# A decode kernel's TensorE program made shorter: looped query projection and query broadcasts, the broadcasts moved behind the MLP's first layer, and branch hints at the end of two engines' programs

## The chip, the cores and the metric

One core of a Trainium2 chip (trn2). The metric is the device time of one execution in microseconds, lower is better. Before: 1292.9 us (median of three: 1292.82, 1292.90, 1293.01).

Ratios between two kernels are computed as the mean time of one kernel's runs over that of the other's runs of the same rounds, so they are not quite the ratio of the medians quoted beside them.

## The reference, cut to what matters

One decode step for batch 8: attention over a key and a value cache beside an MLP, both on a layer norm of the same `x`.

```python
xn = layernorm(x)                                 # (8, 1, 576)
q  = (xn @ wq).reshape(B, 1, 32, 128)             # 32 heads of 128
p  = softmax(einsum(q, k_cache) * 128**-0.5)      # k_cache, v_cache: (8, 32, 4096, 128) bf16
a  = einsum(p, v_cache).reshape(B, 1, 4096) @ wo
h  = gelu(layernorm(xn) @ w1 + b1)                # 576 -> 4608
return x + a + h @ w2 + b2
```

The caches are 2 x 268 MB and are read once. Everything else is small.

## The kernel before: the parts that matter

The cache goes through in 32 tiles. Each tile has one key load and one value load of 8 MB (64 KB on each of 128 partitions), all issued by SyncE on one DMA queue into a ring that also holds, at the start, the weights and scratch of the head. The head is everything ahead of the first tile: layer norms, query projection, query broadcasts, the MLP's first layer with its activation, and a turn of the hidden vector.

```python
# SyncE's order of loads (cut)
load wq; load w1; load_kv(k_v, 0, 0)              # issued at once, traffic until about 44 us
wait(wq_read, head_done); load_kv(v_v, 0, 1)      # value load 0
wait(mlp_done)                                    # the next keys overwrite w1 and the head's scratch
for t in range(1, NT):
    sy.wait_ge(sem["kf"], NX * (t - 1) + 2)       # two key blocks of tile t-1 are used
    load_kv(k_v, t, 0)
    sy.wait_ge(sem["vf"], t)                      # values of tile t-1 are used
    load_kv(v_v, t, 1)
```

So the load of keys 1 waits for the start of tile 0, and the load of values 1 for its end. From tile 1 on, the tiles wait for their keys instead: VectorE's wait for keys is 281.3 us in 31 pieces, the longest 9.1 us (list of waits).

```python
# TensorE in the head (cut)
def queries(e):                                   # 36 matmuls, 32 columns each, four side by side
    for c in range(WC):
        for m in range(M):
            e.matmul(S_ps[0][m*MP:(m+1)*MP, :], lhsT=xT[:, c, :], rhs=wv[:, m], ...)
...
for b in range(B):                                # broadcasts: 8 x 4 matmuls, 64 columns each
    for v in range(2):
        for k in range(NG):
            e.matmul(t[k*M*QP:(k+1)*M*QP, v*NH2:(v+1)*NH2, :], lhsT=sel[:, v*B+b], rhs=q_v[:, k], ...)
    # ScalarE copies the bank to qb
... then the first layer, waiting for w1; activation; turn; then VectorE's first key product
```

The softmax here doesn't subtract the row's maximum and nothing guards it: scores larger than these inputs give would overflow.

Of the kernel before, what the change touches and what calls it, by code (L numbers as in the profile page):

```python
# [3 lines left out]
ALU = mybir.AluOpType  # L4
# [5 lines left out]
P = 128  # L10
# [4 lines left out]
QP = P // G  # L15
# [99 lines left out]
def later(src, dst, engine):  # L115

    ins = list(src.instructions)
    wait = next(i for i in ins if i.engine == engine and type(i).__name__ == "InstEventSemaphore")
    assert not dst.instructions
    src.instructions = [i for i in ins if i is not wait]  # L120
    dst.instructions = [wait]


def decode(nc, A_x, A_k_cache, A_v_cache, A_wq, A_wo, B_x, B_w1, B_b1, B_w2, B_b2, out):
# [68 lines left out]
    bv = sb("bv", [2, MP], BF16)  # L193
# [25 lines left out]
    HS, HJ = 3, 2  # L219
    HK = R // (HS * HJ)  # L220
    assert HS * HJ * HK == R and HK * P <= NB
# [4 lines left out]
    xT = early(0, [P, WC, MP])  # L226
    sel = early(0, [P, 2 * B, M, QP])
    q = early(0, [P, NB])
    yT = early(1, [P, WC, MP])
    b1r = early(1, [2, HF])  # L230
    t1s = [early(1, [HS * MP, HK, P], FP32) for _ in range(HJ)]
    hs = [early(1, [HS * MP, HK, P]) for _ in range(HJ)]
# [7 lines left out]
    o_ps, tot_ps, oT_ps = bank("o_ps"), bank("tot_ps"), bank("oT_ps")  # L240
    acc = [bank(f"acc{m}") for m in range(NO)]

    names = ["k", "v", "prod", "ebd", "ob", "s", "o", "t", "sc", "x", "rec", "kf", "vf", "on", "end", "out"]
# [4 lines left out]

    def block(name, eng=ENG.PE):

        nc.enter_bb(name, parent=main, valid_engines=[eng])

# [32 lines left out]
    od.op("gpsimd", [], ["xT"], lambda e: e.memset(xT, 0.0))  # L285
    od.op("gpsimd", [], ["yT"], lambda e: e.memset(yT, 0.0))
    od.op("gpsimd", [], ["bv"], lambda e: e.memset(bv[:], 0.0))
# [74 lines left out]

    def queries(e):
        for c in range(WC):
            wv = wq_sb[:, c, :].rearrange("p (x m d) -> p m x d", m=M, d=Dh)
            for m in range(M):
                i = e.matmul(
                    S_ps[0][m * MP:(m + 1) * MP, :], lhsT=xT[:, c, :], rhs=wv[:, m],
                    start=(c == 0), stop=(c == WC - 1))
        return i  # L370
# [15 lines left out]
    q_v = q.rearrange("r (n k d) -> r k n d", n=NH2, k=NG)  # L386
    for b in range(B):
        ps, key = (tot_ps, "tot") if b % 2 else (oT_ps, "oT")
        t = ps.rearrange("p (g d) -> p g d", d=Dh)

        def broadcast(e, t=t, b=b):
            for v in range(2):
                for k in range(NG):
                    i = e.matmul(
                        t[k * M * QP:(k + 1) * M * QP, v * NH2:(v + 1) * NH2, :],
                        lhsT=sel[:, v * B + b].rearrange("p m q -> p (m q)"), rhs=q_v[:, k],
                        start=True, stop=True)
            return i

        pe(["q", "sel"], [key], broadcast)  # L400
        dst = qb[:, b * NHG:(b + 1) * NHG, :]
        act([key], [f"qb{b}"], lambda e: e.activation(out=dst, in_=t, func=ACT.Copy))

# [3 lines left out]
    h_ps = [p[:HS * MP, :HK * P].rearrange("p (k r) -> p k r", k=HK) for p in (o_ps, S_ps[2])]  # L407

    def layer(e, lhsT, rows, **flags):
        wv = rows.rearrange("x (p r) -> x r p", r=R)  # L410
        for j in range(HJ):
            for s in range(HS):
                r0 = (s * HJ + j) * HK
                i = e.matmul(  # L414
                    h_ps[j][s * MP:(s + 1) * MP], lhsT=lhsT, rhs=wv[:, r0:r0 + HK, :], **flags)
        return i
# [4 lines left out]
    pe(["bv", "b1r"], ["h_ps"], lambda e: layer(e, bv[:], b1r, start=False, stop=True))  # L421
    for j in range(HJ):
        t1, k1, hp, h = t1s[j], f"t1_{j}", h_ps[j], hs[j]
        act(["h_ps"], [k1], lambda e: e.activation(out=t1, in_=hp, func=ACT.Square))  # L424
        dve([k1], [k1], lambda e: e.tensor_scalar(  # L425
            out=t1, in0=t1, scalar1=0.044715, scalar2=1.0, op0=ALU.mult, op1=ALU.add))
        dve([k1, "h_ps"], [k1], lambda e: e.tensor_tensor(out=t1, in0=t1, in1=hp, op=ALU.mult))
        act([k1], [k1], lambda e: e.activation(out=t1, in_=t1, func=ACT.Tanh, scale=GELU_C))
        dve([k1], [k1], lambda e: e.tensor_scalar(
            out=t1, in0=t1, scalar1=1.0, scalar2=0.5, op0=ALU.add, op1=ALU.mult))  # L430
        dve([k1, "h_ps"], [f"h{j}"], lambda e: e.tensor_tensor(
            out=h, in0=t1, in1=hp, op=ALU.mult))
    for j in range(HJ):
        h = hs[j]
        t = S_ps[j][:, :HK * HS * MP].rearrange("p (k n) -> p k n", k=HK)

        def turn(e, h=h, t=t):
            for k in range(HK):
                i = e.matmul(
                    t[:, k, :], lhsT=h[:, k, :], rhs=ident[:HS * MP, :HS * MP],  # L440
# [5 lines left out]
            out=hT_sb[:].rearrange("p (s j k) n -> p j k s n", s=HS, j=HJ)[:, j],  # L446
            in_=t.rearrange("p k (s n) -> p k s n", s=HS)[:, :, :, :2 * B]))
# [51 lines left out]
    ve, sa, te = nc.vector, nc.scalar, nc.tensor  # L499
# [110 lines left out]
    sa.sem_inc(sent)  # L610

# [65 lines left out]
    block("project")  # L677

# [25 lines left out]
    ins.then_inc(sem["end"], 1)  # L704

# [25 lines left out]
```

## Time and profile before

From the page of the kernel before: the span, and part 3, which has for each DMA queue its packets, bytes, and the time that they took as a share of sixteen engines' span.

```profile
span 1291.5 us, 14658 instructions
...
q1 hardware_dynamic: 10368, 556.93, 99.7%
q8 instruction: 3, 0.05, 0.0%
...
q14 instruction: 1, 0.01, 0.0%
```

Queue 1, with all the loads, fills the DMA engines for 99.7% of the span: this kernel is bound by its traffic. I took it that an engine's work costs time only where it delays a load; r5 below agrees, where 11.5 us more work of VectorE cost 4.6 us. The lines "instruction" I read as fetches of program text, since they come and go with the program: with the hints added (r2) queue 8 has two packets instead of three and queue 14 none. They look like nothing, but the packet records below show otherwise.

From the timeline of the kernel before (start us, duration us, engine line operation, tiles, count, and in brackets the idle time before it): the queries, the first and the last four broadcasts, one group of the layer, the first key product, and loads.

```profile
13.84 4.01 PE L367 MATMUL s_ps<-ring 128*32 128x512 bf16 x36 [1.36 <-DVE quad L354]
...
18.55 0.41 PE L394 MATMUL oT_ps<-ring 128*64 128x256 bf16 x4 [0.36 <-ACT ring L385]
...
22.57 0.64 PE L394 MATMUL tot_ps<-ring 128*64 128x256 bf16 x4
...
23.95 0.33 SPq L271 DMA_DIRECT2D ring<-in_A_v_cache_dram  x1
...
26.02 0.85 PE L414 MATMUL o_ps<-ring 128*32 128x384 bf16 x3 [2.80 <-DMA ring<-in_B_w_dram]
...
46.82 6.70 DVE L559 TENSOR_TENSOR ring<-ring,qb 128x4096 bf16<-128x4096 bf16 x3 [0.32 <-DVE hT_sb L445]
...
53.53 0.33 SPq L271 DMA_DIRECT2D ring<-in_A_k_cache_dram  x1
...
74.24 0.33 SPq L271 DMA_DIRECT2D ring<-in_A_v_cache_dram  x1
```

The queries' narrow matmuls start four at a time (the first four within 0.01 us, at 13.84 us), the broadcasts two at a time (the first two within 0.01 us, at 18.55 us). The first layer starts at 26 us because its weights land then (bracket). The broadcasts and ScalarE's copies of them, 18.6 to 23.9 us, lie in that wait. Keys 1 are issued at 53.5 us.

The chain that ended last, in order of time (start us, duration us, what):

```profile
1259.74 28.52 DMA ring<-in_A_wo_dram
1288.26 0.04 issue
1288.31 1.29 PE acc L374 x18
1289.60 0.02 issue
1289.62 0.45 DVE fin L604
```

The time is set by the landing of the last weights; about 4.4 us follow.

**The packet records.** The trace also has each DMA packet's start and duration. A load ends with sixteen packets of 4 bytes (1136 for the 71 loads), which I read as one on each of the sixteen engines, so one can see when each engine finished it. Worked out from these records for the kernel before:

- Steady state: an 8 MB load takes each engine 19.35 us (8.39 MB: 433 GB/s), and load follows load without a gap.
- Thirteen engines finish each load within 0.5 us of one another. Three are 1.2 to 1.4 us behind them, to the end. They fall behind one at a time, each after an instruction fetch: at 29.9 us (queue 8, 16384 bytes, 1.02 us), 52.2 us (queue 14, 8192 bytes, 0.31 us) and 76.0 us (queue 8, 16384 bytes, 1.05 us). The records do not name the engine of a packet; that an engine delayed once stays behind is read from lags that repeat load after load: 1.32, 1.42 and 1.54 us behind the median at 102.5 us, 1.35, 1.45 and 1.57 us at 1244 us.
- The last weights' final packets: thirteen engines by 1287.1 us, the three late ones at 1288.3 to 1288.5 us.

### The profile page before, as it was taken

To read this page: it belongs to the slowest core of one execution; us is meant where nothing else is said; L and a number is where in the kernel's file an instruction comes from. 1 tells how busy PE (TensorE), PEld (TensorE's weight loads), DVE (VectorE), ACT (ScalarE), POOL (GpSimd) and SP (SyncE) were. 2 spreads that over 40 slices of the span, in tenths; PEclk is the share of its full clock that TensorE was granted. 3 is DMA by queue.
4 is the path that set the end of the run, shared out by engine and by line. 5 is a ranking of instruction groups with operands and counts; after the bars stand their busy time and mean duration, and the time that the engine had idled before them with its cause. 6 is when DMAs were issued, how large, how long until landed. Compare 5 with 4: busy or idle time off the path is not lost. (4 is left out here: it accounts for less than half of the span.)

```text
span 1291.5 us, 14658 instructions
## 1 busy us (share of the span) xinstructions
PE 736.8 (57%) x4707; PEld 322.3 (25%) x4707; DVE 829.4 (64%) x740; ACT 56.8 (4%) x181; POOL 2.4 (0%) x12
## 2 busy tenths in 40 slices
PE   4654565554565554665554565554566554565557
PEld 1222232222222222222222232222222222222223
DVE  2655677655677655677655677655677655577654
ACT  2000000000000000000000000000000000000000
POOL 0000000000000000000000000000000000000000
PEclk8778887778887777887777887778887777888779
DMA  9999999999999999999999999999999999999998
GB/s 419 441 427 440 430 428 449 422 428 449 422 428 449 422 430 447 422 436 440 424 436 438 426 438 434 428 442 428 428 449 422 428 449 422 428 449 422 430 447 350
DMA packets 10410, 557.02 MB, mean 431 GB/s; under 512 B 1163, under 2 KB 1188, under 8 KB 1446
## 3 DMA queue, kind: packets, MB, share of 16 engines
q1 hardware_dynamic: 10368, 556.93, 99.7%
q8 instruction: 3, 0.05, 0.0%
q10 hardware_dynamic: 38, 0.02, 0.0%
q14 instruction: 1, 0.01, 0.0%
HBM read 556.94 MB, written 0.01 MB: 431 GB/s over the span
## 5 line engine op out<-in xcount | busy, mean ns | idle before, releaser
L643 PE MATMUL s_ps<-ring,ident 128*128 x2048 | 544.5, 423 | 514.1 <-PEq L641 513.1
L559 DVE TENSOR_TENSOR ring<-ring,qb 128x4096 bf16<-128x4096 bf16 x256 | 579.2, 2283 | 281.6 <-DMA ring<-in_A_k_cache_dram 281.3
L643 PEld LDWEIGHTS s_ps<-ring,ident 128*128 128x128 bf16 x2048 | 217.4, 106 | 828.3 <-issue 678.5
L534 DVE TENSOR_REDUCE sc<-s_ps 128x32 f32<-128x512 f32 x256 | 171.8, 684 | 0.0
L662 PE MATMUL o_ps<-ring,ebd 128*32 128x512 bf16 x2048 | 116.4, 380 | 0.0
L546 DVE TENSOR_TENSOR ebd<-es,head 128x1536 bf16<-128x1536 bf16 x64 | 77.9, 1218 | 0.0
L569 DVE RECIPROCAL rec<-tot_ps 128x8 f32<-128x8 f32 x32 | 6.6, 208 | 110.7 <-PE oT_ps L670 110.7
L582 ACT ACTIVATE es<-sc 128x192 bf16<-128x192 f32 x64 | 19.8, 310 | 1104.2 <-DVE sc L534 1104.2
L662 PEld LDWEIGHTS o_ps<-ring,ebd 128*32 128x32 bf16 x2048 | 51.6, 97 | 62.5 <-issue 13.6
L670 PE MATMUL oT_ps<-selc,ob 128*128 128x8 f32 x256 | 33.9, 259 | 12.3 <-ACT ob L586 12.3
L670 PEld LDWEIGHTS oT_ps<-selc,ob 128*128 128x128 f32 x256 | 31.0, 191 | 15.2 <-ACT ob L586 15.2
L586 ACT ACTIVATE ob<-o_ps 128x512 f32<-128x512 f32 x32 | 19.1, 597 | 80.2 <-PE o_ps L662 80.2
L425 DVE TENSOR_SCALAR ring<-ring 96x384 f32<-96x384 f32 x2 | 0.7, 352 | 26.4 <-ACT ring L424 26.4
L545 DVE TENSOR_TENSOR Es<-Ep 128x1 f32<-128x1 f32 x32 | 5.1, 160 | 13.3 <-ACT es L582 13.3
L666 PEld LDWEIGHTS tot_ps<-headf,Es 128*128 128x128 f32 x64 | 9.5, 187 | 13.6 <-issue 13.6
L666 PE MATMUL tot_ps<-headf,Es 128*128 128x8 f32 x64 | 12.4, 266 | 0.0
L582 ACT ACTIVATION_READ_ACCUMULATOR es<-sc 128x1 f32 x64 | 11.9, 186 | 0.0
L414 PE MATMUL o_ps<-ring 128*32 128x384 bf16 x27 | 7.8, 860 | 2.8 <-DMA ring<-in_B_w_dram 2.8
L574 DVE TENSOR_TENSOR Ox<-on,quad 128x32 bf16 x32 | 6.2, 192 | 4.8
L414 PE MATMUL s_ps<-ring 128*32 128x384 bf16 x27 | 7.9, 862 | 0.0
L374 PE MATMUL acc<-ring,hT_sb 128*8 128x288 bf16 x72 | 6.0, 335 | 2.8 <-DMA ring<-in_B_w_dram 2.8
L336 PE MATMUL tot_ps<-ident,ring 40*128 40x16 bf16 x9 | 0.7, 204 | 11.8 <-DVE ring L314 11.8
(76 smaller groups left out, 61.2 us busy)
## 6 DMA issues: line engine op xcount, KB each, us to landing
ring<-in_B_w_dram SPq DMA_DIRECT2D x2, 5184.0 KB, 25.2
ring<-in_A_wq_dram SPq DMA_DIRECT2D x1, 4608.0 KB, 13.7
ring<-in_A_wo_dram SPq DMA_DIRECT2D x1, 1728.0 KB, 28.6
ring<-in_A_wo_dram SPq DMA_DIRECT2D x1, 1584.0 KB, 26.5
ring<-in_A_wo_dram SPq DMA_DIRECT2D x1, 1008.0 KB, 28.5
ring<-in_A_k_cache_dram SPq DMA_DIRECT2D x32, 31.9
ring<-in_A_v_cache_dram SPq DMA_DIRECT2D x32, 30.5
ring<-in_A_wo_dram SPq DMA_DIRECT2D x1, 288.0 KB, 28.8
```

The source lines that it names most:

```text
L414: i = e.matmul(h_ps[j][s * MP:(s + 1) * MP], lhsT=lhsT, rhs=wv[:, r0:r0 + HK, :], **flags)
L534: ins = ve.tensor_reduce(out=sc[:, n * CB:(n + 1) * CB], in_=bank_of(x).rearrange("p (c d) -> p c d", d=DL), axis=AX.X, op=ALU.add)
L546: ve.tensor_tensor(out=ebd[:, ja:jb], in0=es[:, a:b].rearrange("p (j c) -> p j c", c=4).unsqueeze(2) .to_broadcast([P, nj, G, 4]), in1=hea ...
L559: ve.tensor_tensor(out=k, in0=k, in1=qb[:, bass.ds(t, 1), :].to_broadcast([P, CB, Dh]), op=ALU.mult,).then_inc(sem["prod"], 1)
L569: ve.reciprocal(out=rec[:], in_=tot_ps[:, :G]).then_inc(sem["rec"], 1)
L574: ve.tensor_tensor(out=Ox[:, bass.ds(t, 1)].rearrange("p o g m -> p (o g) m"), in0=on[:].unsqueeze(2).to_broadcast([P, G, M]), in1=quad[:] ...
L582: sa.activation(out=es[:, a * CB:b * CB], in_=sc[:, a * CB:b * CB], func=ACT.Exp, scale=scale, accum_out=Ep[:, i:i + 1]).then_inc(sem["x"], 1)
L586: sa.activation(out=ob[:].rearrange("r c d -> r (c d)"), in_=o_ps, func=ACT.Copy).then_inc(sem["ob"], 1)
L643: ins = te.matmul(to, lhsT=idn, rhs=k[:, :, d * DL:(d + 1) * DL], start=(d == 0), stop=(d == Dh // DL - 1))
L662: ins = te.matmul(o_ps[m * MP:(m + 1) * MP, :], lhsT=ebd[:, j].rearrange("p g c -> p (g c)"), rhs=vals[:, c:c + 4, :], start=(j < M), stop ...
L666: te.matmul(tot_ps[:, :G], lhsT=Es[:].to_broadcast([P, P]), rhs=headf[:], start=True, stop=True).then_inc(sem["vf"], 1)
L670: ins = te.matmul(oT_ps[:, :G], lhsT=ob[:, c, :], rhs=selc[:, c, :], start=(c == 0), stop=(c == 3))
```

## The change

The intent: fewer instructions in TensorE's program, by loops with register addresses in place of unrolled code. The looped matmuls are widened with zeros, the queries to full width; looped matmuls at the old width were not run (r4 and r16 go back to it unrolled). The broadcasts go behind the first layer, where ScalarE and VectorE compute the activation. Two hints name the last branch of VectorE and of TensorE.

```diff
     def queries(e):
-        for c in range(WC):
-            for m in range(M):
-                i = e.matmul(S_ps[0][m * MP:(m + 1) * MP, :], lhsT=xT[:, c, :], rhs=wv[:, m], ...)
+        def part(at, w, start):                     # zeros around the 32 columns: 128 wide
+            for m in range(M):
+                e.matmul(S_ps[0], lhsT=xTz[:, bass.ds(at + (M - 1 - m) * MP, P)], rhs=wv[:, m], ...)
+        part(0, 0, True)
+        (at, w), close = looped("queries", WC - 1, at=(M * MP, M * MP), w=(HQ, HQ))
+        part(at, w, False)
+        close()
 ...
-    for b in range(B): ...                          # 32 unrolled broadcasts, before the layer
     ... first layer (now in groups of 4 x 512 and 1 x 256 columns, not 6 x 384) ...
+    def broadcasts(e):                              # behind the layer, a loop of 8
+        (at,), close = looped("broadcast", B, at=(0, MQ))
+        e.wait_ge(sem["free"], 1).then_inc(sem["free"], -1)
+        for v in range(2):
+            for k in reversed(range(NG)):
+                i = e.matmul(t[:(k + 1) * MQ, v * NH2:(v + 1) * NH2, :],
+                    lhsT=selz[:, bass.ds(at + (v * B + 1 - k) * MQ, (k + 1) * MQ)], rhs=q_v[:, k], ...)
+        i.then_inc(sem["full"], 1)
+        close()
+    ... squares; queries_out(range(2)); tanh ...; queries_out(range(2, B)); turn
 ...
+    vector_last = nc.mark_branch_hint_location(ENG.DVE)     # at the start of VectorE's program
+    ve.br("vector_end").branch_hint(vector_last)            # at its end
+    place = nc.mark_branch_hint_location(ENG.PE)            # at the start of the projection
+    te.br("tensor_end").branch_hint(place)                  # at TensorE's end
```

More of the change, by code (lines that the diff above doesn't have):

```diff
@@ L117, in later @@
     ins = list(src.instructions)
-    wait = next(i for i in ins if i.engine == engine and type(i).__name__ == "InstEventSemaphore")
+    moved = [next(i for i in ins if i.engine == engine and type(i).__name__ == kind)
+             for kind in ("InstDrain", "InstEventSemaphore")]
     assert not dst.instructions
-    src.instructions = [i for i in ins if i is not wait]
-    dst.instructions = [wait]
+    src.instructions = [i for i in ins if i not in moved]
+    dst.instructions = moved
 def decode(nc, A_x, A_k_cache, A_v_cache, A_wq, A_wo, B_x, B_w1, B_b1, B_w2, B_b2, out):
@@ L192, in decode @@
     low = sb("low", [P, MP], BF16)
-    bv = sb("bv", [2, MP], BF16)
     stats = {t: sb(f"stats_{t}", [B, 2, nc.vector.BN_STATS_DIM], FP32) for t in "xy"}
@@ L217, in early, with between @@
         return t
-    HS, HJ = 3, 2
-    HK = R // (HS * HJ)
-    assert HS * HJ * HK == R and HK * P <= NB
+    def between(room, groups, n):
+        pad = (groups - 1) * MP
+        t = early(room, [P, pad + n * groups * MP])
+        return t, t[:, pad:].rearrange("p (c r) -> p c r", c=n)[:, :, :MP]
+    HK = NB // P
+    HG = [(j, s, r, min(r + HK, R)) for n, r in enumerate(range(0, R, HK)) for j, s in [divmod(n, M)]]
+    HJ = HG[-1][0] + 1
+    HN = [[(r0, r1) for j, _, r0, r1 in HG if j == i] for i in range(HJ)]
+    assert all(len({r1 - r0 for r0, r1 in g}) == 1 for g in HN)
+    HR = [(len(g), g[0][1] - g[0][0], g[0][0]) for g in HN]
     x8, b2r = early(0, [B, D]), early(0, [1, D])
@@ L225, in decode @@
     dup = early(0, [YP + B, D, 2])
-    xT = early(0, [P, WC, MP])
-    sel = early(0, [P, 2 * B, M, QP])
-    q = early(0, [P, NB])
+    xTz, xT = between(0, M, WC)
+    MQ = M * QP
+    selz = early(1, [P, (1 + 2 * B) * MQ])
+    sel = selz[:, MQ:].rearrange("p (i m q) -> p i m q", m=M, q=QP)
+    q = early(1, [P, NB])
     yT = early(1, [P, WC, MP])
+    bv = early(1, [2, MP])
     b1r = early(1, [2, HF])
-    t1s = [early(1, [HS * MP, HK, P], FP32) for _ in range(HJ)]
-    hs = [early(1, [HS * MP, HK, P]) for _ in range(HJ)]
+    t1s = [early(1, [n * MP, k, P], FP32) for n, k, _ in HR]
+    hs = [early(1, [n * MP, k, P]) for n, k, _ in HR]
     def bank(name):
@@ L239, in decode @@
     S_ps = [s_all[:, i * NB:(i + 1) * NB] for i in range(NS)]
-    o_ps, tot_ps, oT_ps = bank("o_ps"), bank("tot_ps"), bank("oT_ps")
+    o_ps = bank("o_ps")
+    b_all = nc.alloc_psum_tensor("b_ps", [P, 2 * NB], FP32)[:]
+    oT_ps, tot_ps = b_all[:, :NB], b_all[:, NB:]
     acc = [bank(f"acc{m}") for m in range(NO)]
-    names = ["k", "v", "prod", "ebd", "ob", "s", "o", "t", "sc", "x", "rec", "kf", "vf", "on", "end", "out"]
+    names = ["k", "v", "prod", "ebd", "ob", "s", "o", "t", "sc", "x", "rec", "kf", "vf", "on", "end", "out", "free", "full"]
     sem = {n: nc.alloc_semaphore(f"m_{n}") for n in names}
@@ L247, in decode @@
     main = nc.cur_bb
+    te = nc.tensor
     def block(name, eng=ENG.PE):
         nc.enter_bb(name, parent=main, valid_engines=[eng])
+    vector_last = nc.mark_branch_hint_location(ENG.DVE)
     wq_sb = ring[:, 0:WQ_END].rearrange("p (c f) -> p c f", c=WC)
@@ L284, in decode @@
     od.op("gpsimd", [], ["dup"], lambda e: e.memset(dup, 0.0))
-    od.op("gpsimd", [], ["xT"], lambda e: e.memset(xT, 0.0))
+    od.op("gpsimd", [], ["xT"], lambda e: e.memset(xTz, 0.0))
     od.op("gpsimd", [], ["yT"], lambda e: e.memset(yT, 0.0))
-    od.op("gpsimd", [], ["bv"], lambda e: e.memset(bv[:], 0.0))
+    od.op("gpsimd", [], ["bv"], lambda e: e.memset(bv, 0.0))
+    od.op("gpsimd", [], ["sel"], lambda e: e.memset(selz[:, :MQ], 0.0))
     def dve(reads, writes, emit):
@@ L360, in decode, with looped, close, nothing @@
         in_=ident[:2, :2].unsqueeze(2).to_broadcast([2, 2, B])))
+    def looped(name, n, **steps):
+        regs = {k: nc.alloc_registers(f"{name}_{k}", engines=[ENG.PE]) for k in steps}
+        for k, (first, _) in steps.items():
+            nc.regs_mov(regs[k], first)
+        te.br(name)
+        block(name)
+        def close():
+            for k, (_, step) in steps.items():
+                nc.regs_alu(regs[k], regs[k], step, op=ALU.add)
+            k, (first, step) = next(iter(steps.items()))
+            te.br_lt(regs[k], first + n * step, on_true=name, on_false=name + "_end")
+            block(name + "_end")
+        return [te.snap(regs[k].handles[0], min_val=f, max_val=f + (n - 1) * st)
+                for k, (f, st) in steps.items()], close
+    def nothing(e, out, lhsT, z):
+        return e.matmul(out, lhsT=lhsT, rhs=z[:, :1], start=False, stop=True)
     def queries(e):
-        for c in range(WC):
-            wv = wq_sb[:, c, :].rearrange("p (x m d) -> p m x d", m=M, d=Dh)
+        def part(at, w, start):
+            wv = ring[:, bass.ds(w, HQ)].rearrange("p (x m d) -> p m x d", m=M, d=Dh)
             for m in range(M):
-                i = e.matmul(
-                    S_ps[0][m * MP:(m + 1) * MP, :], lhsT=xT[:, c, :], rhs=wv[:, m],
-                    start=(c == 0), stop=(c == WC - 1))
-        return i
+                e.matmul(
+                    S_ps[0], lhsT=xTz[:, bass.ds(at + (M - 1 - m) * MP, P)], rhs=wv[:, m],
+                    start=start and m == 0, stop=False)
+        part(0, 0, True)
+        (at, w), close = looped("queries", WC - 1, at=(M * MP, M * MP), w=(HQ, HQ))
+        part(at, w, False)
+        close()
+        return nothing(e, S_ps[0][:, :1], idn, xTz)
     def accumulate(e, lhsT, rhs, start=False, stop=False):
@@ L385, in decode @@
     act(["s0"], ["q"], lambda e: e.activation(out=q, in_=S_ps[0], func=ACT.Copy))
-    q_v = q.rearrange("r (n k d) -> r k n d", n=NH2, k=NG)
-    for b in range(B):
-        ps, key = (tot_ps, "tot") if b % 2 else (oT_ps, "oT")
-        t = ps.rearrange("p (g d) -> p g d", d=Dh)
-        def broadcast(e, t=t, b=b):
-            for v in range(2):
-                for k in range(NG):
-                    i = e.matmul(
-                        t[k * M * QP:(k + 1) * M * QP, v * NH2:(v + 1) * NH2, :],
-                        lhsT=sel[:, v * B + b].rearrange("p m q -> p (m q)"), rhs=q_v[:, k],
-                        start=True, stop=True)
-            return i
-        pe(["q", "sel"], [key], broadcast)
-        dst = qb[:, b * NHG:(b + 1) * NHG, :]
-        act([key], [f"qb{b}"], lambda e: e.activation(out=dst, in_=t, func=ACT.Copy))
     head_done = [od.last(e) for e in ("tensor", "vector", "scalar")]
-    h_ps = [p[:HS * MP, :HK * P].rearrange("p (k r) -> p k r", k=HK) for p in (o_ps, S_ps[2])]
+    h_ps = [p[:n * MP, :k * P].rearrange("p (k r) -> p k r", k=k)
+            for p, (n, k, _) in zip((o_ps, S_ps[2]), HR)]
     def layer(e, lhsT, rows, **flags):
         wv = rows.rearrange("x (p r) -> x r p", r=R)
-        for j in range(HJ):
-            for s in range(HS):
-                r0 = (s * HJ + j) * HK
-                i = e.matmul(
-                    h_ps[j][s * MP:(s + 1) * MP], lhsT=lhsT, rhs=wv[:, r0:r0 + HK, :], **flags)
+        for j, s, r0, r1 in HG:
+            i = e.matmul(h_ps[j][s * MP:(s + 1) * MP], lhsT=lhsT, rhs=wv[:, r0:r1, :], **flags)
         return i
@@ L420, in decode, with queries_out @@
             e, yT[:, c, :], w1_sb[:, c, :], start=(c == 0), stop=False))
-    pe(["bv", "b1r"], ["h_ps"], lambda e: layer(e, bv[:], b1r, start=False, stop=True))
-    for j in range(HJ):
-        t1, k1, hp, h = t1s[j], f"t1_{j}", h_ps[j], hs[j]
+    pe(["bv", "b1r"], ["h_ps"], lambda e: layer(e, bv, b1r, start=False, stop=True))
+    q_v = q.rearrange("r (n k d) -> r k n d", n=NH2, k=NG)
+    nc.scalar.sem_inc(sem["free"], 2)
+    def broadcasts(e):
+        to = nc.alloc_registers("broadcast_to", engines=[ENG.PE])
+        nc.regs_mov(to, 0)
+        (at,), close = looped("broadcast", B, at=(0, MQ))
+        t = b_all[:, bass.ds(te.snap(to.handles[0], min_val=0, max_val=NB), NB)].rearrange(
+            "p (g d) -> p g d", d=Dh)
+        e.wait_ge(sem["free"], 1).then_inc(sem["free"], -1)
+        for v in range(2):
+            for k in reversed(range(NG)):
+                i = e.matmul(
+                    t[:(k + 1) * MQ, v * NH2:(v + 1) * NH2, :],
+                    lhsT=selz[:, bass.ds(at + (v * B + 1 - k) * MQ, (k + 1) * MQ)], rhs=q_v[:, k],
+                    start=True, stop=True)
+        i.then_inc(sem["full"], 1)
+        nc.regs_alu(to, NB, to, op=ALU.subtract)
+        close()
+        return e.wait_ge(sem["free"], 2)
+    assert NG == 2
+    pe(["q", "sel"], ["oT", "tot"], broadcasts)
+    def queries_out(rows):
+        for b in rows:
+            nc.scalar.wait_ge(sem["full"], b + 1)
+            nc.scalar.activation(
+                out=qb[:, b * NHG:(b + 1) * NHG, :], func=ACT.Copy,
+                in_=(oT_ps, tot_ps)[b % 2].rearrange("p (g d) -> p g d", d=Dh)
+            ).then_inc(sem["free"], 1)
+    ts = [(t1s[j], f"t1_{j}", h_ps[j], hs[j], f"h{j}") for j in range(HJ)]
+    for t1, k1, hp, _, _ in ts:
         act(["h_ps"], [k1], lambda e: e.activation(out=t1, in_=hp, func=ACT.Square))
@@ L427, in decode @@
         dve([k1, "h_ps"], [k1], lambda e: e.tensor_tensor(out=t1, in0=t1, in1=hp, op=ALU.mult))
+    queries_out(range(2))
+    for t1, k1, hp, h, hk in ts:
         act([k1], [k1], lambda e: e.activation(out=t1, in_=t1, func=ACT.Tanh, scale=GELU_C))
@@ L430, in decode, with turn @@
             out=t1, in0=t1, scalar1=1.0, scalar2=0.5, op0=ALU.add, op1=ALU.mult))
-        dve([k1, "h_ps"], [f"h{j}"], lambda e: e.tensor_tensor(
+        dve([k1, "h_ps"], [hk], lambda e: e.tensor_tensor(
             out=h, in0=t1, in1=hp, op=ALU.mult))
-    for j in range(HJ):
+    queries_out(range(2, B))
+    for j, (n, k, r0) in enumerate(HR):
         h = hs[j]
-        t = S_ps[j][:, :HK * HS * MP].rearrange("p (k n) -> p k n", k=HK)
-        def turn(e, h=h, t=t):
-            for k in range(HK):
+        t = S_ps[j][:, :k * n * MP].rearrange("p (k n) -> p k n", k=k)
+        def turn(e, h=h, t=t, n=n, k=k):
+            for c in range(k):
                 i = e.matmul(
-                    t[:, k, :], lhsT=h[:, k, :], rhs=ident[:HS * MP, :HS * MP],
+                    t[:, c, :], lhsT=h[:, c, :], rhs=ident[:n * MP, :n * MP],
                     start=True, stop=True)
@@ L445, in decode @@
         dve([f"s{j}"], [f"hT{j}"], lambda e: e.tensor_copy(
-            out=hT_sb[:].rearrange("p (s j k) n -> p j k s n", s=HS, j=HJ)[:, j],
-            in_=t.rearrange("p k (s n) -> p k s n", s=HS)[:, :, :, :2 * B]))
+            out=hT_sb[:, r0:r0 + n * k].rearrange("p (s k) n -> p k s n", s=n),
+            in_=t.rearrange("p k (s n) -> p k s n", s=n)[:, :, :, :2 * B]))
     mlp_done = [od.last(e) for e in ("tensor", "vector", "scalar")]
@@ L497, in bank_of @@
         return S_ps[x % NS]
-    ve, sa, te = nc.vector, nc.scalar, nc.tensor
+    ve, sa = nc.vector, nc.scalar
     fin_d, fin_a, sent = (nc.alloc_semaphore(n) for n in ("fin_d", "fin_a", "sent"))
@@ L610, in decode @@
     sa.sem_inc(sent)
+    ve.br("vector_end").branch_hint(vector_last)
+    block("vector_end", ENG.DVE)
     block("head")
@@ L704, in decode @@
     ins.then_inc(sem["end"], 1)
+    te.br("tensor_end").branch_hint(place)
+    block("tensor_end")
 _INS = ['A_x', 'A_k_cache', 'A_v_cache', 'A_wq', 'A_wo', 'B_x', 'B_w1', 'B_b1', 'B_w2', 'B_b2']
```

## The prediction

> **What bounds the kernel.** The page's DMA table puts queue 1 at 99.7% of sixteen engines' span: 556.9 MB. From its first packet at 1.0 us to the last weight piece at about 1288.3 us that is 433 GB/s[...]. The engines have slack: in the list of waits VectorE waits 281 us in 31 pieces (9.1 us a tile) for keys. The chain of waits ends: last projection weights land, 18 matmuls from 1288.31 (1.29 us), copies (0.45 us), output DMA, SyncE's end at 1291.5; the measured time is 1.4 us longer than the span.
>
> **What decides the last landing.** I read the trace's DMA packet records. Every load is split evenly over sixteen engines which never run dry, so an engine that is delayed stays behind. Thirteen engines finish each load within 0.5 us; three come 1.2 to 1.4 us later, to the end. They fall behind one by one, after three instruction fetches: 16 KB on queue 8 at 29.9 us (took 1.02 us), 8 KB on queue 14 at 52.2 us, 16 KB on queue 8 at 76.0 us. A fourth fetch (queue 8, 1287.1 us) fell on an engine already done; a fifth (queue 14, 8 KB) comes at 1291.6 us, after the kernel's last work.[...]
>
> **What the change does.** TensorE's stream shrinks from 791 instructions (counted in the built program) to 676. Its head falls from about 305 to about 190[...]. In-stream fetches are moved, not all removed: I expect two or three engines still 1 to 1.4 us late, and the last landing within 0.3 us of before.
> The query matmuls now write all 128 columns, one after another: before, 36 took 4.0 us; now about 8 to 9 us, ending near 23 us, before the first-layer weights land (26.0 us). Broadcasts, 5.3 us before the layer, now follow it, and the copies (0.60 us each) interleave with the activation. Estimate: first key product 1 to 4 us later than 46.8 us, the next key load at about 56 us instead of 53.5 us. The queue holds work until about 65 us, so nothing dries up; the 9 us of slack per tile absorbs the rest. Worth zero.
> End hints: the fetch at 1291.6 us should move earlier, which may cut up to about 0.6 us of the 1.4 us behind the span.
>
> **Prediction:** 1292.3 us, 1291.2 to 1293.2 eight times in ten; faster by over 2%: 0.005, within 2%: 0.99, slower: 0.005.
>
> **What would show it.** Right: queue 1 still above 99%; the queries' matmuls about twice as long; first key product at 48 to 51 us; queue-8 fetches two in number (around 50 to 75 us, and around 1280 us); last landing near 1288.3 us; no fetch right after the last instruction; gain, if any, behind the span. Wrong: if no engine lags at the end, the last landing comes at 1287.1 us and the time falls by about 1 us more (TensorE then still has 46 matmuls until 1287.4 us). If two fetches hit one engine, or the hints fetch in mid-stream, an engine is 2 us late and the kernel is about 1 us slower. If the head is longer by over 12 us, the queue dries at 65 us and each further microsecond costs one.

How the sum comes to 1292.3 us: 1292.9 us of the kernel before, nothing for the moved fetches, nothing for the longer head, and 0.6 us less for the hints at the end. The 0.6 us and the outcomes under "Wrong" are estimates from the trace: the fetch at 1291.6 us takes 0.53 us and ends 0.6 us behind the span; a fetch of 16384 bytes takes 1.02 us and left an engine 1.2 to 1.4 us late; thirteen engines finish the last weights by 1287.1 us, the three late ones by 1288.5 us; the load in front of keys 1 ends at 63.5 to 65.3 us. The rate of 433 GB/s stands as measured; that no higher one can be had is not shown, and the fetches' new places (around 50 to 75 us and around 1280 us) stand as my guess.

## The result, and the profile after

The changed kernel: 1293.57 us (median of six: 1292.93, 1294.20, 1294.54, 1292.90, 1292.74, 1296.30) against 1292.91 us (six, 1292.82 to 1293.04). Ratio 1.0008, 95% interval 0.9995 to 1.0021: the same within 2%, but 0.4 us above the predicted range, and uneven, where the kernel before is not.

The page after, span and queues:

```profile
span 1291.4 us, 14772 instructions
...
q1 hardware_dynamic: 10368, 556.93, 99.8%
...
q8 instruction: 1, 0.02, 0.0%
```

Queue 8 has one fetch left in the span instead of three, and queue 14's is gone. Its timeline, answering to the one above:

```profile
13.65 10.14 PE L410 MATMUL s_ps<-ring 128*128 128x512 bf16 x36 [1.40 <-DVE quad L375]
...
24.54 0.33 SPq L291 DMA_DIRECT2D ring<-in_A_v_cache_dram  x1
...
25.92 1.08 PE L443 MATMUL o_ps<-ring 128*32 128x512 bf16 x4 [1.78 <-DMA ring<-in_B_w_dram]
...
39.76 5.51 PE L465 MATMUL b_ps<-ring 128*128 128x256 bf16 x16
...
46.22 5.50 PE L465 MATMUL b_ps<-ring 128*128 128x256 bf16 x16 [0.95 <-PEq L462]
...
53.96 6.70 DVE L624 TENSOR_TENSOR ring<-ring,qb 128x4096 bf16<-128x4096 bf16 x3 [0.32 <-DVE hT_sb L510]
...
60.68 0.33 SPq L291 DMA_DIRECT2D ring<-in_A_k_cache_dram  x1
...
81.38 0.33 SPq L291 DMA_DIRECT2D ring<-in_A_v_cache_dram  x1
```

The queries take 10.1 us instead of 4.0 us, which the layer does not feel: it still starts when its weights land (25.92 us). The 32 broadcasts run one after another, 0.34 us each (5.51 us for 16), from 39.8 to 51.7 us. The first key product comes at 53.96 us, 7.1 us later than before, and with it the loads of keys 1 and values 1.

Busy time by stretch in the kernel after (stretch, its length, then busy us and count of TensorE, its weight loads, VectorE, ScalarE and GpSimd, granted TensorE clock, DMA share, GB/s):

```profile
26.00:38.00 12.00, 12.00 (x45) 1.92 (x44) 0.00 (x0) 0.00 (x0) 0.00 (x0) 1.00 1.01 437
38.00:46.00 8.00, 7.27 (x22) 1.97 (x21) 2.52 (x6) 4.83 (x9) 0.00 (x0) 0.54 0.91 393
46.00:54.00 8.00, 6.25 (x22) 2.33 (x22) 1.47 (x6) 2.77 (x5) 0.00 (x0) 0.50 1.00 434
```

The clock (third column from the right) falls to one half at 38.6 us, about as the broadcasts begin, and stays there until 62.5 us. TensorE was busy 12.00 of the 12 us before; the ends of matmuls are modelled in the profile, and what lowered the clock is not shown. Each broadcast costs 0.34 us at that clock; in r7 below the same matmuls also run at the full clock, and start 0.22 us apart there.

The chain at the end is the same five steps, 0.1 us earlier:

```profile
1259.65 28.51 DMA ring<-in_A_wo_dram
1288.16 0.04 issue
1288.20 1.29 PE acc L422 x18
1289.49 0.02 issue
1289.52 0.45 DVE fin L669
```

So removing two of the three in-stream fetches and making the head 7 us longer together moved the last landing by 0.1 us in this execution. That is two terms which cancel, as the table below shows: the slowest engine is 1.29 us instead of 1.57 us behind, and 0.30 us are lost where the load of keys 1 follows. Why other executions take 1.3 to 3.4 us longer does not show in this trace.

### The profile page after: what moved, and what is told of

Same layout as the page of the kernel before. It is cut to its first block, busy times and chain, and to the rows that moved or that the text cites. A ratio compares the mean times of both kernels' runs of the same rounds, so it can differ in the third digit from the quotient of the medians.

```text
span 1291.4 us, 14772 instructions
## 1 busy us (share of the span) xinstructions
PE 742.5 (57%) x4698; PEld 325.4 (25%) x4698; DVE 829.4 (64%) x740; ACT 56.6 (4%) x181; POOL 3.3 (0%) x13
## 5 line engine op out<-in xcount | busy, mean ns | idle before, releaser
L710 PE MATMUL s_ps<-ring,ident 128*128 x2048 | 536.8, 418 | 514.6 <-PEq L708 514.6
L634 DVE RECIPROCAL rec<-b_ps 128x8 f32<-128x8 f32 x32 | 6.6, 208 | 110.7 <-PE b_ps L737 110.7
L737 PE MATMUL b_ps<-selc,ob 128*128 128x8 f32 x256 | 33.9, 259 | 12.3 <-ACT ob L651 12.3
L737 PEld LDWEIGHTS b_ps<-selc,ob 128*128 128x128 f32 x256 | 31.0, 191 | 15.2 <-ACT ob L651 15.2
L443 PE MATMUL o_ps<-ring 128*32 128x512 bf16 (+1 forms) x40 | 12.8, 1079 | 1.8 <-DMA ring<-in_B_w_dram 1.8
L733 PEld LDWEIGHTS b_ps<-headf,Es 128*128 128x128 f32 x64 | 9.5, 187 | 13.6 <-issue 13.6
L733 PE MATMUL b_ps<-headf,Es 128*128 128x8 f32 x64 | 12.4, 267 | 0.0
L465 PE MATMUL b_ps<-ring 128*128 128x256 bf16 (+1 forms) x32 | 11.0, 409 | 0.9 <-PEq L462 0.9
L410 PE MATMUL s_ps<-ring 128*128 (+1 forms) x36 | 10.1, 453 | 1.4 <-DVE quad L375 1.4
```

Source lines behind the costliest of these rows:

```text
L410: e.matmul(S_ps[0], lhsT=xTz[:, bass.ds(at + (M - 1 - m) * MP, P)], rhs=wv[:, m], start=start and m == 0, stop=False)
L443: i = e.matmul(h_ps[j][s * MP:(s + 1) * MP], lhsT=lhsT, rhs=wv[:, r0:r1, :], **flags)
L465: i = e.matmul(t[:(k + 1) * MQ, v * NH2:(v + 1) * NH2, :], lhsT=selz[:, bass.ds(at + (v * B + 1 - k) * MQ, (k + 1) * MQ)], rhs=q_v[:, k], ...
L710: ins = te.matmul(to, lhsT=idn, rhs=k[:, :, d * DL:(d + 1) * DL], start=(d == 0), stop=(d == Dh // DL - 1))
L733: te.matmul(tot_ps[:, :G], lhsT=Es[:].to_broadcast([P, P]), rhs=headf[:], start=True, stop=True).then_inc(sem["vf"], 1)
L737: ins = te.matmul(oT_ps[:, :G], lhsT=ob[:, c, :], rhs=selc[:, c, :], start=(c == 0), stop=(c == 3))
```

## The experiments

I first held theory Q: the longer head has used up the time by which the loads of keys 1 and values 1 were issued early, so the queue runs dry there, and whatever makes the head later is paid in full. The rival F: it is the instruction fetches and hints. In the first expectation I wrote that thirteen engines had been idle for 0.45 us at 63.4 us in the first trace. That was a misreading of finishing times; the packet records show all engines occupied there, with longer packets (below).

The 95% intervals of the ratios below are 0.13 to 0.17% (1.7 to 2.2 us) wide on each side, so that most of them hold 1; r5, r6 and r9 are the ones that do not. Tenths of a microsecond are read from traces and from the spread of executions, and are no stronger than that.

Three quantities from the packet records are used; a seam is the point where an engine passes from one load to the next. "Seam loss": the median over the engines of the time at which they finish a load, minus the same for the load before, minus the steady 19.35 us. "Slowest behind": how far the slowest engine is behind that median late in the stream (the load finished near 1244 us). "Last landing": the last weights' final packet.

| trace | keys 1 issued | values 1 issued | seam losses | slowest behind | last landing | time minus span | time |
|---|---|---|---|---|---|---|---|
| before | 53.5 | 74.2 | 0.00, 0.00 | 1.57 | 1288.54 | 1.36 | 1292.88 |
| before + hints | 53.5 | 74.2 | 0.00, 0.01 | 1.74 | 1288.77 | 1.37 | 1293.12 |
| after, packed broadcasts | 55.9 | 77.0 | 0.00, 0.00 | 1.29 | 1288.58 | 1.52 | 1293.10 |
| after, first | 60.7 | 81.4 | 0.30, 0.00 | 1.29 | 1288.41 | 1.51 | 1292.93 |
| after, r14 | 60.8 | 81.5 | 0.43, 0.00 | 0.76 | 1288.08 | 1.52 | 1292.61 |
| after, r15 | 60.5 | 81.2 | 0.06, 0.04 | 2.12 | 1289.24 | 1.37 | 1293.63 |
| after, r17 | 60.4 | 81.4 | 0.08, 0.09 | 1.08 | 1288.48 | 2.53 | 1294.04 |
| after, no hints | 60.7 | 81.4 | 0.18, 0.07 | 1.24 | 1289.01 | 1.37 | 1293.35 |
| after, broadcasts first | 62.2 | 83.2 | 0.26, 1.55 | 0.87 | 1289.92 | 2.15 | 1295.11 |
| before + 11.5 us | 65.0 | 85.7 | 2.89, 1.45 | 0.61 | 1292.56 | 1.37 | 1296.92 |
| after + 4.9 us | 65.6 | 86.3 | 3.47, 1.46 | 0.77 | 1292.80 | 1.65 | 1297.44 |
| before + 18.4 us | 71.6 | 92.6 | 9.46, 1.70 | 0.93 | 1299.02 | 1.37 | 1303.40 |

### r1: the changed kernel again

No edit.

> The changed kernel once more, for the spread of its executions. Theory Q (queue runs dry): in the first trace the second key load was issued at 60.7 us (before: 53.5 us), and thirteen of sixteen DMA engines then sat idle for about 0.45 us at 63.4 us; anything that makes the head later still costs one for one. The head's 36 query matmuls and 32 broadcast matmuls run one after another at a clock of 1.0 or 0.5, so executions should differ: 1292.7 to 1296.5 us, and in any trace the time over 1292.9 us should equal the delay of that issue beyond about 60.7 us. Rival F (instruction fetch and hints): executions differ through fetches; a slow trace would show fetches in other places and the issue unmoved.

Measured: 1293.3 us (five, 1292.89 to 1293.48) against 1292.93 us; ratio 1.0001, 0.9988 to 1.0015. No execution above 1294 us this time. The issues stood at 60.6 and 81.5 us, as in the first trace. Seam losses 0.05 and 0.25 us: the loss is at the other seam. One part of the expectation failed: the traced execution took 1293.45 us with the issue unmoved.

### r2: the hints alone, on the kernel before

```diff
+    vector_last = nc.mark_branch_hint_location(ENG.DVE)
 ...
+    ve.br("vector_end").branch_hint(vector_last)
+    place = nc.mark_branch_hint_location(ENG.PE)     # start of the projection
+    te.br("tensor_end").branch_hint(place)
```

> Kernel before plus the two end hints alone. Theory Q: time within 0.3 us of before (1292.9 us) and as tight (range under 0.5 us), since the head is unchanged; the fetches at 52 us (queue 14) and 1287 us (queue 8) should be gone as they are in the changed kernel's trace, but two queue-8 fetches near 30 and 76 us stay, so engines still end 1.2 to 1.4 us late. Rival F (hints make executions uneven): spread of over 1 us.

Measured: 1293.07 us (1292.92 to 1293.22) against 1292.93; ratio 1.0001, 0.9987 to 1.0014. Both fetches named are gone, as expected: the page has two of queue 8 and no line for queue 14.

```profile
q1 hardware_dynamic: 10368, 556.93, 99.7%
q8 instruction: 2, 0.03, 0.0%
q10 hardware_dynamic: 38, 0.02, 0.0%
```

In the packet records two engines instead of three are over 1 us late. The landing is set by the slowest engine (1.74 us behind with two late, 1.57 us with three; last landings 1288.77 and 1288.54 us), so two late ones cost as much as three. The fetch of 8192 bytes after the last instruction is still there (1292.1 us), and time minus span is 1.37 us as before (1.32 to 1.42 us in its five executions, 1.31 to 1.55 us in those of the kernel before). The hints are worth nothing here: the 0.6 us that I had given them at the end did not come.

### r3: the changed kernel without the hints

The four hint lines of the diff taken out.

> Changed kernel without the two end hints. Theory Q: as uneven as the changed kernel (1292.7 to 1296.5 us), median within 1 us of it; the fetch of queue 14 near 52 us comes back, and perhaps one of queue 8 near 1282 us, which would add 0 to 1 us. Rival F: tight again, near 1292.9 us.

Measured: 1293.67 us (1293.35 to 1294.25) against 1292.93; ratio 1.0006, 0.9993 to 1.002. The fetch of queue 14 is back at 59.2 us, and a queue-8 fetch appears at 1282.0 us, where I had predicted it (around 1280 us) for the changed kernel. Another engine is then 2.1 us behind the first to finish on the next load, where the slowest had been 1.6 us, and the last landing is 1289.01 us. So with the head's change, the hints do one useful thing: without them a fetch falls just ahead of the end.

### r4: the broadcasts unrolled and narrow again, still behind the layer

```diff
-        (at,), close = looped("broadcast", B, at=(0, MQ)) ... t[:(k + 1) * MQ, ...], lhsT=selz[:, bass.ds(...)]
+        for b in range(B):
+            for v in range(2):
+                for k in range(NG):
+                    i = e.matmul(t[k * MQ:(k + 1) * MQ, v * NH2:(v + 1) * NH2, :],
+                                 lhsT=sel[:, v * B + b], rhs=q_v[:, k], ...)
```

> Changed kernel with the broadcasts unrolled and 64 columns wide as before, still behind the first layer (about 50 TensorE instructions more). Theory Q: broadcasts end by about 47 us instead of 52 us, first key product at 48 to 50 us, second key load issued before 57 us, no dry queue: 1292.0 to 1292.9 us and a range under 0.6 us. Rival F: as uneven as the changed kernel, 1292.7 to 1296 us.

Measured: 1292.90 us (1292.63 to 1293.24) against 1292.93; ratio 0.9999, 0.9985 to 1.0013. From its timeline:

```profile
46.22 1.13 PE L460 MATMUL b_ps<-ring 128*64 128x256 bf16 x8 [0.30 <-PEq L457]
...
49.59 6.70 DVE L617 TENSOR_TENSOR ring<-ring,qb 128x4096 bf16<-128x4096 bf16 x3 [0.32 <-DVE hT_sb L503]
55.93 0.33 SPq L291 DMA_DIRECT2D ring<-in_A_k_cache_dram  x1
```

Eight narrow broadcast matmuls take 1.1 us where eight wide ones take 2.75 us (half of 5.5 us), at the same halved clock. The first key product comes 4.4 us earlier than in the changed kernel (49.59 against 53.96 us), and both seam losses are gone. But its program of 741 instructions has a queue-8 fetch at 1278.6 us, and two engines end about 1 us behind the rest. So: no seam loss, more lateness from fetches, same time. The other 2.8 us of the head's 7.1 us are still there (49.59 against 46.82 us). They arise behind the layer, which ends at 40 us in both kernels: here broadcasts and copies share TensorE and ScalarE with the activation, where before they lay in the wait for the layer's weights. What the layer's new grouping adds to that was not run apart.

### r5, r6: the kernel before with a later head

```diff
     mlp_done = [od.last(e) for e in ("tensor", "vector", "scalar")]
+    for _ in range(5):                               # r6: 8
+        dve(["head", "delay"], ["delay"], lambda e: e.tensor_tensor(out=ebd[:], in0=hh, in1=hh, op=ALU.mult))
```

These write a buffer that is not yet in use; nothing else changes.

> Kernel before with five idle-making VectorE operations (about 1.6 us each by scaling the 1.22 us operation of 1536 elements) between the first-layer work and the first key product, nothing else changed: first key product near 55 us, second key load issued near 61.5 us, about as late as in the changed kernel. Theory Q: the slack is used up just here; thirteen engines idle for about 1 us at 63.5 us, the three late ones hide most of it: 1292.9 to 1293.7 us. Rival F (fetches decide): 1292.9 us, unmoved.

> The same with eight operations (about 13 us): second key load near 66.4 us. Theory Q: beyond the slack each microsecond costs one, so about 4.9 us more than with five: 1297 to 1299 us. Rival (VectorE's 9 us of slack in every tile absorbs it): 1292.9 to 1293.5 us.

Measured: r5 1297.68 us (1296.92 to 1298.02), r6 1303.99 us (1303.40 to 1305.36), against 1293.04 us (1292.68 to 1293.34). Ratios 1.0037 (1.0021 to 1.0054) and 1.0089 (1.0072 to 1.0106). The operations took 2.3 us each, not 1.6 us, so the delays were 11.5 and 18.4 us and my figures for the times are too low. From r5's timeline:

```profile
46.38 11.59 DVE L452 TENSOR_TENSOR ebd<-head 128x2048 bf16<-128x2048 bf16 x5
58.28 6.70 DVE L563 TENSOR_TENSOR ring<-ring,qb 128x4096 bf16<-128x4096 bf16 x3 [0.32 <-DVE ebd L452]
...
65.00 0.33 SPq L271 DMA_DIRECT2D ring<-in_A_k_cache_dram  x1
...
85.70 0.33 SPq L271 DMA_DIRECT2D ring<-in_A_v_cache_dram  x1
```

A head later by 11.5 us costs 4.6 us of time, one later by 18.4 us costs 10.95 us. Between the two, 6.9 us of delay cost 6.3 us: nearly one for one. The part that was free is 11.5 - 4.6 = 6.9 us, or 18.4 - 10.95 = 7.4 us. The changed kernel's head is 7.1 us later: it has spent just about all of it.

### r7: the order undone alone (looped broadcasts before the layer)

```diff
-    for c in range(WC): pe(["yT", "w1"], ["h_ps"], ...)     # layer
     pe(["q", "sel"], ["oT", "tot"], broadcasts)
+    queries_out(range(B))
+    for c in range(WC): pe(["yT", "w1"], ["h_ps"], ...)     # layer
```

> Changed kernel with the order undone alone: the looped broadcasts again before the first layer. The clock was 1.0 from 18 to 38 us in the changed kernel's trace, so the broadcasts should take 6 to 8 us there instead of 12, but the layer starts near 31 us instead of 26 us: first key product at 51 to 54 us, second key load at 58 to 61 us; theory Q: 1292.7 to 1293.5 us, and more even than the changed kernel if the load is issued before 60 us.

Measured: 1294.48 us (1293.87 to 1295.11) against 1293.04; ratio 1.0010, 0.9993 to 1.0027. The first key product comes at 55.73 us, outside what I expected, and so is the time:

```profile
26.03 0.95 PE L460 MATMUL b_ps<-ring 128*128 128x256 bf16 x4 [0.38 <-PEq L457]
...
27.33 8.16 PE L460 MATMUL b_ps<-ring 128*128 128x256 bf16 x24 [0.35 <-PEq L457]
...
36.27 1.08 PE L443 MATMUL o_ps<-ring 128*32 128x512 bf16 x4 [0.78 <-ACT qb L474]
...
55.73 6.70 DVE L623 TENSOR_TENSOR ring<-ring,qb 128x4096 bf16<-128x4096 bf16 x3 [0.32 <-DVE hT_sb L509]
62.20 0.33 SPq L291 DMA_DIRECT2D ring<-in_A_k_cache_dram  x1
```

The clock went to one half at 27.6 us here, so most broadcasts take 0.34 us each in this place too (8.16 us for 24); the eight before that, at the full clock, start 0.22 us apart (four in 0.95 us, the last one's end included). The layer starts 10 us late. So, given looped queries, which end at 23.5 us and leave no room before the weights land, and looped broadcasts, the changed order is the better one, by 1.8 us of head. And these 1.8 us more of head are paid for: 1.4 us above the kernel before, where the changed kernel in r1 was 0.4 us above it, with a seam loss of 1.55 us at values 1.

### r9, r10, r11: the changed kernel with a later head, and two looks at it

The edit of r5 with two operations, in the changed kernel.

> Changed kernel with two of the same VectorE operations before the first key product (2.3 us each as measured, so about 4.6 us later). Theory Q: the changed kernel stands at the edge, so the time rises by nearly all of it: second key load near 65.2 us, 1296.8 to 1298.5 us, and every unevenness of the head shows in the time. Rival (the changed kernel still has some us of slack): 1293 to 1295 us.

> The same, one look: with the slack gone, time and issue of the second key load should move together from look to look, within 0.5 us; what differs earlier in the head (the granted clock's phase, the landing of the inputs, a fetch) names the source of the unevenness.

> The same, a second look, for the same comparison: time and issue of the second key load move together within 0.5 us.

Measured: r9 1297.09 us (1296.46 to 1298.34) against 1293.00; ratio 1.0032, 1.0016 to 1.0049. Looks: 1296.50 and 1297.84 us. The first key product came at 58.86 us, 4.9 us later than in the changed kernel, and the time is 4.1 us above the kernel before: so of 4.9 us about 0.8 us were free (1.1 us if counted from 1293.28 us, the median of all 22 executions of the changed kernel). That is the slack that it has left. Stretches of r9 behind the first value load:

```profile
62.00:64.00 2.00, 2.00 (x7) 0.62 (x6) 2.00 (x2) 0.00 (x0) 0.00 (x0) 0.50 0.03 8
64.00:66.00 2.00, 2.00 (x6) 0.74 (x5) 2.00 (x2) 0.00 (x0) 0.00 (x0) 0.50 0.00 0
66.00:68.00 2.00, 2.00 (x9) 0.84 (x8) 2.00 (x2) 0.00 (x0) 0.00 (x0) 0.81 1.49 524
```

A packet is counted where it starts, and the ones of the value load last until about 64.7 us; between 64 and 66 us no data packet of a load starts at all (DMA share 0.00), until the keys issued at 65.57 us. This is the dry queue of theory Q.

The other half of what I expected failed. Time and issue did not move together: the issues were 65.57, 65.33 and 65.48 us, within 0.24 us, and the times 1297.44, 1296.50 and 1297.84 us, 1.34 us apart. The head did not vary; what varied came later. The packet records say what: the slowest engine is 0.50 us behind the median in the fastest execution and 1.37 us in the slowest. So the engines come out of the seams unequally, and the lag stays. I call this theory Q2: a load issued so late leaves some engine further behind, and that engine sets the last landing.

### r8, r12, r13, r14, r15, r17, r18: more looks at the changed kernel

No edit. In search of a slow execution.

> The changed kernel, one look in search of a slow execution (three of eleven took 1294.2 to 1296.3 us). Theory Q: if the time is above 1294 us, the second key load or the value load behind it is issued later than in the first trace (60.7 and 81.4 us) by about the excess. Rival F: issues unmoved, a fetch elsewhere or an engine 2 us or more behind.

> The changed kernel, another look for a slow execution. Theory Q: above 1294 us only with the second key load later than 61.5 us or the value load behind it later than 82.3 us.

> The changed kernel, a look for a slow execution. Theory Q1 (a late head): above 1294 us only with the second key load issued after 61.5 us or the value load behind it after 82.3 us. Theory Q2 (the seam): the issues are unmoved, and the excess appears at the seam behind one of these two loads, where some DMA engine falls 1 us or more further behind for good. Rival F: the excess comes with a fetch away from a seam, or behind the last landing.

> The changed kernel, a further look, same three expectations: late issue (Q1), engine left behind at a seam (Q2), or a fetch away from a seam (F).

> The changed kernel, a further look, same three expectations: late issue (Q1), engine left behind at a seam (Q2), or a fetch away from a seam (F).

> The changed kernel once more, for the spread on another occasion and one more trace. Theory Q2 (seam): 1292.6 to 1294.5 us, the kernel before within 0.6 us; in the trace, time minus last landing stays at 4.3 to 4.8 us and the excess, if any, is an engine left behind at 63 or 83 us with the loads issued at 60.5 to 61.1 and 81.2 to 81.7 us.

> The changed kernel, a last look, same expectations: time minus last landing 4.3 to 4.8 us; any excess is an engine left behind at one of the two seams (Q2), or a late issue (Q1).

Measured: looks at 1292.90, 1292.86, 1293.26, 1292.61, 1293.63 and 1293.29 us (r8, r12 to r15, r18). r17: 1293.69 us (five, 1292.52 to 1294.04) against 1292.93 us (nine, 1292.71 to 1293.23); ratio 1.0003, 0.9989 to 1.0016. In all nine traces of the changed kernel keys 1 were issued at 60.0 to 61.0 us and values 1 at 81.2 to 81.6 us. Four things vary between them instead:

- The seams. Between 62 and 67 us, 15 of 30 full packets of the first trace took over 2.5 us, up to 4.0 us (keys 1 were issued there 2.7 us ahead of the first engine's end of the load in front); in the kernel before none of 32 did (median 2.42 us). In r1 it was 5 of 31 there, and 9 of 30 between 81.5 and 86.5 us. The two seam losses add up to 0.1 to 0.5 us in the nine traces, and to 0.0 us before and in r4.
- The slowest engine. From 0.76 us (r14, the fastest trace) to 2.12 us behind the median. In r15 the slowest engine is 1.3 us behind the median when it finishes keys 1 and 2.2 us when it finishes values 1, although both loads were issued early there (60.5 and 81.2 us); the last landing is 1289.24 us and the time 1293.63 us. That is Q2, with the issues unmoved.
- The fetch. The one in-stream fetch (queue 8) starts at 58.6 to 58.9 us in six of the nine traces and at 61.3 us, one packet of 2.42 us later, in three (r1, r13, r15). The last landings of the three are 1288.5 to 1289.2 us, those of the six 1288.1 to 1288.8 us. I did not test whether this matters. It is a rival to Q2 for part of the lag, but not for the 0.9 us of r15, which come at the seam of values 1, where no fetch is.
- The end. r17's traced execution is a slow one, 1294.04 us, yet its span is 1291.5 us and its last landing 1288.48 us. The DMA view for the time behind its last instruction:

```profile
DMA packets 1, 0.02 MB, mean 5 GB/s; under 512 B 0, under 2 KB 0, under 8 KB 0
## 3 DMA queue, kind: packets, MB, share of 16 engines
q8 instruction: 1, 0.02, 3.0%
```

A queue-8 fetch of 16384 bytes starts at 1292.85 us and takes 1.42 us; time minus span is 2.53 us instead of 1.4 to 1.7 us. r7's trace has the same (fetch at 1294.4 us, 2.15 us). The kernel before makes its third queue-8 fetch at 1287.1 us, ahead of its end, and has 1.36 us. In r15 it starts at 1291.30 us, inside the span, and costs nothing there (1.37 us). So rival F has a part after all: in some executions that fetch is left for the very end, 0.6 to 1.0 us dearer. It would account for r17's unevenness: its three slowest executions (1293.69, 1293.79 and 1294.04 us) have spans of 1291.5 to 1291.6 us, no longer than those of the kernel before in the same rounds (1291.4 to 1291.8 us), and time minus span of 2.09, 2.29 and 2.54 us. Only the last of them has a trace that shows the fetch. I expected no such thing from r17 (4.3 to 4.8 us between last landing and end; it was 5.6 us).

### r16: the query projection as before, in the changed kernel

```diff
-        part(0, 0, True) ... looped("queries", ...) ... 128 wide
+        for c in range(WC):
+            for m in range(M):
+                i = e.matmul(S_ps[0][m * MP:(m + 1) * MP, :], lhsT=xT[:, c, :], rhs=wv[:, m], ...)
```

> Changed kernel with the query projection alone as before (unrolled, 32 columns wide, four side by side, about 44 TensorE instructions more). Theory Q: queries end near 18 us instead of 23.5 us, but the layer still waits for its weights until 26 us, so the first key product stays at 53 to 55 us and the time at 1292.7 to 1293.5 us. Rival (the looped queries make the head late): first key product at 48 to 50 us.

Measured: one look, 1293.63 us. The first key product stays at 54.09 us: in this order the looped queries have no part in the head's 7 us. The time is just outside what I expected. The program of 734 instructions fetches at 1282.2 us again, and the last landing is 1289.27 us.

## Why the prediction was wrong

It had three parts that could move the time. The first held in the first trace, the other two failed.

1. *"In-stream fetches are moved, not all removed ... the last landing within 0.3 us of before."* Right in the first trace: 1288.41 against 1288.54 us, though with some luck: 0.28 us less lag of the slowest engine and 0.30 us of seam loss, neither of them foreseen, cancelled. The reason held: each in-stream fetch leaves one more engine behind (three before, two in r2 with one fetch fewer, a further one in r3 after the fetch at 1282 us), and the slowest engine decides. How I had got from the shorter program to the fetches' places no trace shows. What I missed: the fetch I placed around 1280 us does not come in the changed kernel. Without the hints (r3) it comes at 1282.0 us, so they suppress it; in the longer programs of r4 and r16 it comes in spite of them (1278.6 and 1282.2 us).
2. *"End hints: ... may cut up to about 0.6 us of the 1.4 us behind the span."* Wrong. Hints alone (r2) changed nothing, 1293.07 against 1292.93 us, and the fetch after the last instruction stayed. In r17 and r7 a larger fetch came there in addition, for 0.6 to 1.0 us. So this term brings no gain and sometimes a loss; with a gain of 0 the estimate is 1292.9 us instead of 1292.3 us.
3. *"First key product 1 to 4 us later ... the next key load at about 56 us ... The queue holds work until about 65 us ... Worth zero."* The mechanism was stated about correctly (once the queue is dry, 6.9 us of delay cost 6.3 us: r5, r6) and both sizes were off. The head grew by 7.1 us: the broadcasts take 12 us where I had carried over the 5.3 us of before, because they run one at a time (0.34 us each), all at half the clock. r4 takes back 4.4 us of the 7.1 us by unrolled narrow broadcasts alone; the 2.8 us that it leaves lie in the predicted 1 to 4 us and come of work behind the layer that was free ahead of it. r16 shows that the queries add nothing in this order, and r7 that going back to the old order would not help as long as queries and broadcasts are looped. The slack was 6.9 to 7.4 us (r5, r6; about 8 us by r9), not the 12 us that I took: I compared the issue of keys 1 (53.5 us) with the latest end of the load in front (65 us). But the binding load is values 1, issued 20.7 us behind keys 1 while the queue advances 19.35 us, and a load needs up to about 2 us from its issue until all engines have a packet of it (the 16th data packet starts 1.6 to 2.3 us after the issue in the eight late loads of r5, r6, r9 and r10). For values 1 before, with 1.9 us as the middle of that: 82.8 - 74.2 - 1.9 = 6.7 us.

So 7.1 us of head met 7 to 8 us of slack, and the changed kernel works at the edge. Its executions are uneven: 1292.52 to 1294.54 us in 21 of 22, against 1292.68 to 1293.34 us in 39 of the kernel before. Their excess lies in two places. Six of the 22 have a longer span than any of the kernel before (1292.0 to 1294.9 us against at most 1291.9 us), which is where losses at the seams would show; three, all of r17, have it behind the span. Half of the executions show neither: the median span is 1291.55 us, the kernel before's 1291.6 us. The median time of all 22 is 1293.28 us (before: 1292.99 us), 0.1 us above the predicted range; that the first six stood at 1293.57 us is in part chance, for they hold the three slowest of the 22.

**What stays open.** The one execution of 1296.30 us, and those of 1294.20 and 1294.54 us, left no trace. Their spans were 1294.9, 1292.8 and 1292.9 us, so their excess lies inside the span, not in a fetch behind it. An engine left behind at a seam fits (r15 shows 0.9 us of it, r9 to r11 show 0.9 us between looks), but no trace shows one of 3 us; the attribution of these three is argued, not shown. Nor is it shown why engines leave a seam unequally, what part the fetch at 61.3 us has in it, or why the fetch behind the span comes in some executions only.

No version tried beats both kernels. r4, with narrow broadcasts, is as even as the kernel before and equal to it.

## What to carry to other kernels

In this kernel, whose one DMA queue is 99.7% busy, work elsewhere was free only until it delayed the issue of a load past the point where the queue still held work: 6.9 to 7.4 us (r5, r6). To estimate that elsewhere: find every load whose issue depends on that work, take the smallest margin (here the next one in the chain was the tighter, values 1, issued 20.7 us behind keys 1 while the queue advanced 19.35 us), and subtract the time from issue to data (here 1.6 to 2.3 us). A fetch of program text in mid-stream cost here what it added to the lag of the slowest DMA engine: with three, two and one such fetches ahead of 1244 us that engine was 1.57, 1.74 and 1.29 us behind (before, r2, r4), so removing some of several gained little. Whether the removal of the last one gains the rest was not run. When an optimisation moves a kernel to the edge of its slack, the median may not tell; compare the spread, and separate what lies inside the span from what lies behind it.
